# Segment sums moved from TensorE to VectorE in a two-branch transformer kernel, with a new order of tiled products and tail

## The chip, the cores and the metric

The kernel runs on one core of a Trainium2 chip. The metric is the device time of one execution, in microseconds (us). A core has five engines with queues of their own, each executed in order: TensorE (PE, matrix products), VectorE (DVE), ScalarE (ACT), GpSimd (POOL) and SyncE (SP), which here only issues transfers (DMA). POOL issues transfers too. Engines wait for one another through semaphores.

## The reference

The output is the sum of three terms on one input `x` of 2048 tokens by 1024 channels, bf16:

```python
xn = _layernorm(x)
return x + A(xn, mem0, Wq, Wk, Wv, Wo, 32) + B(xn, w1, w2, w3, w4)

# A: recurrent memory attention, 32 heads of 128, segments of 32 tokens
for s in range(64):
    h = concat([mem, xn[segment s]])            # 8 memory tokens + 32
    q, k, v = h @ Wq, h @ Wk, h @ Wv
    p = softmax(where(mask, q @ k.T * scale, -1e9))
    o = (p @ v) @ Wo
    mem = o[:8]; outs.append(o[8:])

# B: token-shift mixer and MLP (width 3584)
h  = gelu(layernorm(xn) @ w1); hs = shift(h) @ w2
x1 = xn + hs
out_B = x1 + gelu(layernorm(x1) @ w3) @ w4
```

## The kernel before

The token axis is cut into 16 tiles of 128 tokens (`NT`), the channels into 8 slabs of 128 (`KT`). The schedule is manual: each engine executes its instructions in the order in which the Python code records them, and a tile pool's buffers add waits where a buffer is used again. Matrix products go to PSUM; most take one of four buffers of the tag `mm`, some one of two larger ones ("A", "B").

*Stage 1* (about 10 to 71 us). Groups of two tiles. DVE computes the layer norm statistics and a normalised tile (`ln_stats`, `ln_apply`), and SP transposes it by a DMA (`dma_trans`, L235; the first tiles go through PE). PE multiplies by w1, eight chains per group (`stage1`, L266), and ACT applies GELU into `hT_all`. ACT also normalises `x` in place (`normalise_x`, L245). From it PE makes segment sums: `seg_sums(n)` multiplies each of the eight slabs of a tile by a 128x4 matrix of ones (L261, `psX`), and ACT copies the result to `xs` (L262). The sums of two tiles stand after the first four chains of the group that follows them.

*Stage 2* (71 to 126 us). Products with w2 (L367), addition of `xn`, second layer norm, a DMA transpose of each tile (L381), and a write of `x1` to memory (`R1`).

*Stage 3* (126 to 528 us). Four blocks `tb` of 512 tokens. Half 0 of a block is 28 GELU chains (L556, ACT at L557), half 1 is 8 chains of 28 products with w4 (L574), which DVE adds to `R1` (L575). `load_R1(n)` loads `R1` and x again, lets POOL add them (L480), lets DVE normalise x (L481) and POOL write it to memory (`xn_scratch`, L482), from where the attention later loads it transposed (L503). Between the chains the function `filler(tb, half, i)` puts products of the memory path: `plan` says which chunk of Wv or Wo is used after which chain (chunks 0 to 3 in half 1 of block 0, then on to half 0 of block 2). Chunk products (L425 `psvb`, L446 `psG`) start from `xb`, which is computed from `xs` at the start of stage 3. They yield the approximate memory states `MZ`.

*Attention* (528 us to the end). Four batches `b` of 512 tokens by eight groups of four heads: 32 steps of 12 chains each, four for Q (L617), four for K (L635), four for V (L644). After given chains (`at(c, f)`) a step does the tiled products of earlier steps: `scores(p)` (L668, `psS`) and `soft(p)` of the step before, and `values(pp)` (L708 `psO`, L709 `psE`) of the one before that. `soft` is a row of DVE operations with POOL copies at the end (`PT` L695, `BD` L697). `values` is evicted by DVE (L713, L720) and ACT (L715, `mem_values` L731). Weights come in 1 MB transfers (`need_w`, L489). In batch 0, `wo_sb` is loaded as well, 1 MB per step, right after the K weights of the next step (L908). The output products `psP` (L827) of a batch run in the second step of the next; those of the last batch form the tail, in which `out_part(b, c, h0, h1)` does the heads h0 to h1 of one of eight output parts, and a part that is not finished keeps its `mm` buffer.

Of the kernel before, what the change touches and what calls it, by code (L numbers as in the profile page):

```python
# [21 lines left out]
P = 128  # L22
S = 2048
D = 1024
# [39 lines left out]
def kernel(  # L64
# [79 lines left out]
    xs = spec.tile([P, KT, NSEG], F32)  # L144
    xb = spec.tile([P, KT, NG], BF16)
    m0 = spec.tile([M, D], BF16)
    lnst = spec.tile([P, NT, 4], F32)

    rightx = main.enter_context(ExitStack())
# [14 lines left out]
    with ExitStack() as keepx:  # L164
# [6 lines left out]
        with ExitStack() as p0:  # L171
# [83 lines left out]
                        w = 2 if n == 0 else 4  # L255
                        nc.scalar.copy(xn2Ts[n // 2][:, n % 2, 4 * h + q:4 * h + q + w, :], p3_[:, q:q + w, :])

            def seg_sums(n):
                ps = aux_tile([P, KT, 4], "AB"[n % 2], "psX")
                for k in range(KT):  # L260
                    nc.tensor.matmul(ps[:, k, :], xts[n][:, k * P:(k + 1) * P], segone[:], start=True, stop=True)  # L261
                nc.scalar.copy(xs[:, :, 4 * n:4 * n + 4], ps[:])  # L262

            def w1_part(g, co, ps, ks):
                for k in ks:
                    nc.tensor.matmul(ps, w1_sb[:, k, co * P:(co + 1) * P], xn2Ts[g][:, :, k, :], start=(k == 0), stop=(k == KT - 1))  # L266
# [60 lines left out]
            ln_half(5, 1)  # L327
            dma_trans(4)
            single(3, 0)
            seg_sums(0)  # L330
            seg_sums(1)
            normalise_x(2)
            ln_stats(6)
            ln_apply(5)
# [3 lines left out]
            for g in range(2, NT // 2):  # L338
                nxt = [n for n in (2 * g + 2, 2 * g + 3) if n < NT]
                for n in nxt:  # L340
                    if 6 < n + 1 < NT:
                        ln_stats(n + 1)
                    ln_apply(n)
                    dma_trans(n)
                stage1(g, range(4))
                for n in (2 * g, 2 * g + 1):
                    seg_sums(n - 2)
                    normalise_x(n)
                stage1(g, range(4, KT))
            seg_sums(NT - 2)  # L350
            seg_sums(NT - 1)

        x3_pool = rightx.enter_context(tc.tile_pool(name="x3", bufs=1, side="right"))
        w3b_pool = rightx.enter_context(tc.tile_pool(name="w3b", bufs=1, side="right"))
# [34 lines left out]
    with ExitStack() as p3:  # L389
# [9 lines left out]
        for k in range(KT):  # L399
            nc.tensor.matmul(ps9[:, k, :], m0[:, k * P:(k + 1) * P], eye9[:], start=True, stop=True)  # L400
        nc.vector.tensor_copy(MZ[:, :, 0:M], ps9[:, :, 0:M])
        nc.vector.tensor_tensor(xb[:, :, 0:1], ps9[:, :, M:M + 1], xs[:, :, 0:1], op=ALU.add)
        nc.vector.tensor_copy(xb[:, :, 1:NG], xs[:, :, 1:NG])

        chunks = {}

# [11 lines left out]
        def use_chunk(c):  # L418
            t = chunks.pop(c)
            if c < 8:  # L420
                w = t[:].rearrange("p (k e) -> p k e", k=KT)
                ps = aux_tile([P, 4, NG], "A", "psvb")
                for k in range(KT):
                    for hh in range(4):
                        nc.tensor.matmul(ps[:, hh, :], w[:, k, hh * P:(hh + 1) * P], xb[:, k, :], start=(k == 0 and hh == 0),  # L425
                                         stop=(k == KT - 1), skip_group_check=True)
                vb = vbT[:, c * 4:(c + 1) * 4, :]
                nc.vector.tensor_scalar(vb, ps[:], 1.0 / L, None, op0=ALU.mult)
                sq = ring.tile([P, 4, NG], F32, tag="sq", bufs=1, name="sq")
                nc.gpsimd.tensor_tensor(sq[:], vb, vb, op=ALU.mult)  # L430
                for hh in range(4):
                    if c == 0 and hh == 0:
                        nc.gpsimd.tensor_copy(thr[:], sq[:, 0, :])
                    else:
                        nc.gpsimd.tensor_tensor(thr[:], thr[:], sq[:, hh, :], op=ALU.add)
                if c == 7:
                    nc.gpsimd.tensor_scalar(chk[:, NV + 7:2 * NV], thr[:], TOL2, None, op0=ALU.mult)
                    nc.gpsimd.tensor_copy(chk[:, NV:NV + 7], chk[:, NV + 7:NV + 8].to_broadcast((P, 7)))
                return
            c -= 8  # L440
            w = t[:].rearrange("p (h d) -> p h d", h=4)
            if c == 0:
                psG[0] = aux_tile([P, KT, NG], "B", "psG")
            for hh in range(4):
                for k in range(KT):
                    nc.tensor.matmul(psG[0][:, k, :], w[:, hh, k * P:(k + 1) * P], vbT[:, c * 4 + hh, :],  # L446
                                     start=(c == 0 and hh == 0 and k == 0), stop=(c == 7 and hh == 3), skip_group_check=True)
            if c == 7:
                nc.vector.tensor_copy(MZ[:, :, M:NZ], psG[0][:])
# [1 line left out]
        plan = {}  # L451
        slots = {}
        for i in range(4):
            plan[(0, 1, 2 * i + 1)] = i
            plan[(1, 0, 7 * i + 6)] = 4 + i
            plan[(1, 1, 2 * i + 1)] = 8 + i
            plan[(2, 0, 7 * i + 6)] = 12 + i
        for c in range(16):
            slots[c] = 0 if c < 8 else c % 2

        def filler(tb, ph, i):
            c = plan.get((tb, ph, i))
            if c is None:
                return
            use_chunk(c)
            nx = c + 2 if c >= 8 else c + 1
            if c == 7:
                load_chunk(8, slots[8])
                load_chunk(9, slots[9])
            elif c < 7 or nx < 16:  # L470
                load_chunk(nx, slots[nx])
# [3 lines left out]
        def load_R1(n):  # L475
            R1 = ring.tile([P, D], F32, tag="R1", name="R1")
            nc.sync.dma_start(R1[:], R1_v[:, n, :])
            xt = ring.tile([P, D], BF16, tag="xt", name="xt", bufs=2)
            nc.sync.dma_start(xt[:], x_v[:, n, :])
            nc.gpsimd.tensor_tensor(R1[:], R1[:], xt[:], op=ALU.add)  # L480
            nc.vector.tensor_scalar(xt[:], xt[:], lnst[:, n, 0:1], lnst[:, n, 2:3], op0=ALU.subtract, op1=ALU.mult)  # L481
            nc.gpsimd.dma_start(xn_v[:, n, :], xt[:])  # L482
            R1s[n] = R1

        A = {}
# [65 lines left out]
        for tb in range(4):  # L551
            for f in range(FT):
                ps = mm_tile("ps3")
                w3 = w3a if f < FH else w3b
                for k in range(KT):
                    nc.tensor.matmul(ps[:], w3[:, k, (f % FH) * P:(f % FH + 1) * P], xn3Ts[tb][:, :, k, :], start=(k == 0), stop=(k == KT - 1))  # L556
                nc.scalar.activation(h3T[:, f, :], ps[:], ACTF.Gelu_apprx_tanh)  # L557
                filler(tb, 0, f)
                if f == 20:
                    load_R1(tb * 4)  # L560
            if tb == 0:
                load_chunk(0, 0)
            if tb == 3:
                rightx.close()
                att_open()
            for j in range(4):
                n = tb * 4 + j
                if j < 3:
                    load_R1(n + 1)
                R1 = R1s.pop(n)  # L570
                for ch in range(2):
                    ps = mm_tile("ps4")
                    for f in range(FT):
                        nc.tensor.matmul(ps[:], h3T[:, f, j * P:(j + 1) * P], w4t[f // 4][:, f % 4, ch * 512:(ch + 1) * 512], start=(f == 0), stop=(f == FT - 1))  # L574
                    nc.vector.tensor_tensor(R1[:, ch * 512:(ch + 1) * 512], ps[:], R1[:, ch * 512:(ch + 1) * 512], op=ALU.add)  # L575
                    filler(tb, 1, 2 * j + ch)
                nc.gpsimd.dma_start(R_v[:, n, :], R1[:])
                if tb == 3 and j == 0:
                    att_prep()
# [278 lines left out]
    for i in range(NS):  # L858
# [8 lines left out]
            hooks.setdefault(c, []).append((f, a))  # L867

        if p is not None:
            at(7, scores, p)  # L870
        if pp is not None:
            at(7, values, pp)
            at(10, mem_values, pp)
        if 4 < s.hg and s.b + 1 < NB:
            for k in range(3 * s.hg - 15, min(3 * s.hg - 12, KT)):
# [3 lines left out]
            at(8, first_soft, p)  # L879
            at(11, first_trans, p)  # L880
        if p is not None:
            at(11 if fz else 7, soft, p)
        if pp is not None and pp.b == 0:
            at(1, first_values, pp)
        if s.hg == 1 and s.b > 0:
# [11 lines left out]
        for c in range(12):  # L897
            if c < 4:
# [5 lines left out]
                if c == 3:  # L904
                    if i + 1 < NS:
                        need_w("k", i + 1)
                    if s.b == 0:
                        nc.sync.dma_start(wo_sb[:, hsl(s.hg), :], Wo_v[:, hsl(s.hg), :])  # L908
                    if s.hg == 4 and s.b + 1 < NB:
                        load_xT(s.b + 1)  # L910
            elif c < 8:
                k_chain(s, c - 4)
                if c == 7 and i + 1 < NS:
                    need_w("v", i + 1)
            else:
                v_chain(s, c - 8)
                if c == 11:
                    if s.b == 0:
                        mem_proj(s, "v", VM)
                    if i + 2 < NS:  # L920
                        need_w("q", i + 2)
            for f, a in hooks.get(c, ()):
                f(*a)
        if last:
            b = s.b
            load_Rt(b, 0)
            load_Rt(b, 1)
            hp = H - 4
            scores(s)
            values(p)  # L930
            soft(s)
            out_part(b, 0, 0, hp)
            mem_values(p)
            out_part(b, 1, 0, hp)
            values(s)
            out_part(b, 2, 0, hp)
            mem_values(s)
            out_part(b, 0, hp, H)
            out_part(b, 1, hp, H)
            out_part(b, 2, hp, H)  # L940
            out_chain(b, 3)
            mem_add(b)
            compare(b)
            finite()
# [134 lines left out]
```

## Time and profile before

| | us |
|---|---|
| median of 4 runs (lowest to highest) | 1485.36 (1483.96 to 1486.18) |
| the profiled execution | 1485.04 |
| its span, first to last instruction | 1483.3 |
| PE busy | 1473.0 (99%) |
| DVE busy | 513.9 (35%) |
| ACT busy | 347.0 (23%) |
| POOL busy | 205.4 (14%) |

The profile is of one execution. "L266" is line 266 of the kernel before. The slices of the profile are fortieths of the span, 37 us each, and a digit is the busy share in tenths. "PEld" is the loading of weights into PE, which overlaps its products. A wait is put down to the instruction that ended it, the "releaser"; "issue" stands for time in which the engine waited for nothing that the profile shows. The chain is followed back from the last instruction, at each step to what released it or to the instruction before it on the same engine. "To landing" is the time from the issue of a transfer to its completion.

### The profile page before, as it was taken

To read this page: it belongs to the slowest core of one execution; us is meant where nothing else is said; L and a number is where in the kernel's file an instruction comes from. 1 tells how busy PE (TensorE), PEld (TensorE's weight loads), DVE (VectorE), ACT (ScalarE), POOL (GpSimd) and SP (SyncE) were. 2 spreads that over 40 slices of the span, in tenths; PEclk is the share of its full clock that TensorE was granted. 3 is DMA by queue.
4 is the path that set the end of the run, shared out by engine and by line. 5 is a ranking of instruction groups with operands and counts; after the bars stand their busy time and mean duration, and the time that the engine had idled before them with its cause. 6 is when DMAs were issued, how large, how long until landed. Compare 5 with 4: busy or idle time off the path is not lost.

```text
span 1483.3 us, 28434 instructions
## 1 busy us (share of the span) xinstructions
PE 1473.0 (99%) x12384; PEld 755.7 (51%) x12384; DVE 513.9 (35%) x1194; ACT 347.0 (23%) x887; POOL 205.4 (14%) x479
## 2 busy tenths in 40 slices
PE   8999999999999999999999999999999999999998
PEld 7844444444444456666544444444444444444444
DVE  8183010010110213546441354541255542154452
ACT  5633202103113023333320232220122220032210
POOL 6042131211120201111100000000000000000000
PEclk9999999999999999999999999999999999999999
DMA  8599753454120745565531354541345452245301
GB/s 222 137 272 240 257 192 100 161 169 160 57 106 3 230 138 180 164 205 166 170 112 54 121 171 143 157 143 53 103 148 167 143 157 72 71 141 154 105 17 58
DMA packets 189395, 208.40 MB, mean 141 GB/s; under 512 B 50426, under 2 KB 158074, under 8 KB 189266
## 3 DMA queue, kind: packets, MB, share of 16 engines
q1 hardware_dynamic: 181122, 178.97, 40.2%
q0 software_dynamic: 8144, 27.56, 5.2%
q8 instruction: 99, 1.62, 0.5%
q14 instruction: 30, 0.25, 0.1%
HBM read 170.07 MB, written 25.17 MB: 132 GB/s over the span
## 4 chain that ended last, share of the span: by engine, by line
PE 98%; DVE 1%; DMA 0%; issue 0%; SPq 0%; ACT 0%; POOL 0%; POOLq 0%; DVEq 0%
PE psK L635 15%; PE psP L827 15%; PE psQ L617 15%; PE psV L644 14%; PE ps L556 13%; PE ps L574 13%; PE ps L367 4%; PE ps L266 3%; PE psS L668 1%; PE psO L708 1%; PE psM L653 1%; PE psvb L425 1%; PE psG L446 1%; PE ps L295 0%; DMA x<-in_A_x_dram 0%; PE ps L281 0%
## 5 line engine op out<-in xcount | busy, mean ns | idle before, releaser
L827 PE MATMUL psP<-wo_sb,oX 128*128 128x512 bf16 (+2 forms) x1056 | 222.1, 373 | 0.0
L574 PE MATMUL ps<-w,hT_all 128*128 128x512 bf16 x896 | 195.0, 379 | 0.0
L635 PEld LDWEIGHTS <-w 128*128 128x128 bf16 x1280 | 125.1, 98 | 99.1
L644 PE MATMUL psV<-w,xT 128*128 128x512 bf16 x768 | 170.3, 379 | 0.0
L617 PE MATMUL psQ<-xT,w 128*128 128x512 bf16 x768 | 169.9, 379 | 0.0
L635 PE MATMUL psK<-xT,w 128*128 128x512 bf16 x768 | 169.7, 379 | 0.0
L827 PEld LDWEIGHTS <-oX 128*128 128x128 bf16 x1056 | 101.9, 98 | 118.8
L617 PEld LDWEIGHTS <-w 128*128 128x128 bf16 x1024 | 98.9, 98 | 116.6
L636 ACT CAST K<-psK 128x512 bf16<-128x512 f32 (+1 forms) x160 | 80.4, 502 | 303.0 <-PE psK L635 303.0
L645 ACT CAST V<-psV 128x512 bf16<-128x512 f32 x128 | 74.9, 585 | 289.9 <-PE psV L644 289.8
L574 PEld LDWEIGHTS <-hT_all 128*128 128x128 bf16 x896 | 87.1, 98 | 103.8
L624 DVE TENSOR_TENSOR Q<-psQ,QM 128x512 bf16<-128x512 f32 (+1 forms) x128 | 87.5, 685 | 144.1 <-PE psQ L617 92.3
L557 ACT ACTIVATE hT_all<-ps 128x512 bf16<-128x512 f32 x112 | 66.8, 597 | 283.4 <-PE ps L556 283.4
L644 PEld LDWEIGHTS <-xT 128*128 128x128 bf16 x768 | 74.1, 98 | 84.7
L556 PE MATMUL ps<-xn3T,w3a 128*128 128x512 bf16 x448 | 97.7, 379 | 0.0
L556 PE MATMUL ps<-xn3T,w3b 128*128 128x512 bf16 x448 | 97.7, 379 | 0.0
L713 DVE TENSOR_TENSOR oX<-psE,VM 128x128 bf16<-128x128 f32 x32 | 9.3, 292 | 217.7 <-PE psE L709 217.7
L720 DVE TENSOR_TENSOR oX<-psO,VM 128x96 bf16<-128x96 f32 (+2 forms) x256 | 82.1, 394 | 0.0
L833 DVE TENSOR_TENSOR ot<-psP,Rt 128x512 bf16<-128x512 f32 (+2 forms) x33 | 22.3, 676 | 168.9 <-PE psP L827 166.0
L481 DVE TENSOR_SCALAR xt<-xt,lnst 128x1024 bf16<-128x1024 bf16 x16 | 8.7, 546 | 179.8 <-POOL R L480 179.8
L556 PEld LDWEIGHTS <-w3b 128*128 128x128 bf16 x448 | 43.5, 98 | 52.0
L556 PEld LDWEIGHTS <-w3a 128*128 128x128 bf16 x448 | 43.5, 98 | 51.7
(159 smaller groups left out, 1267.3 us busy)
## 6 DMA issues: line engine op xcount, KB each, us to landing
w<-in_A_Wq_dram SPq DMA_DIRECT2D x32, 1024.0 KB, 5.3
w<-in_A_Wk_dram SPq DMA_DIRECT2D x32, 1024.0 KB, 5.3
w<-in_A_Wv_dram SPq DMA_DIRECT2D x32, 1024.0 KB, 6.5
R_scratch<-x POOLq DMA_DIRECT2D x16, 512.0 KB, 7.9
R<-R_scratch SPq DMA_DIRECT2D x16, 512.0 KB, 7.0
chunk<-in_A_Wv_dram SPq DMA_DIRECT2D x8, 1024.0 KB, 5.5
R_scratch<-R POOLq DMA_DIRECT2D x16, 512.0 KB, 3.9
chunk<-in_A_Wo_dram SPq DMA_DIRECT2D x8, 1024.0 KB, 6.7
```

Source lines behind the costliest of these rows:

```text
L367: nc.tensor.matmul(ps[:], hTB[:, k, o:o + P], w2_sb[:, k, ch * 512:(ch + 1) * 512], start=(k == 0), stop=(k == KT - 1))
L556: nc.tensor.matmul(ps[:], w3[:, k, (f % FH) * P:(f % FH + 1) * P], xn3Ts[tb][:, :, k, :], start=(k == 0), stop=(k == KT - 1))
L557: nc.scalar.activation(h3T[:, f, :], ps[:], ACTF.Gelu_apprx_tanh)
L574: nc.tensor.matmul(ps[:], h3T[:, f, j * P:(j + 1) * P], w4t[f // 4][:, f % 4, ch * 512:(ch + 1) * 512], start=(f == 0), stop=(f == FT - 1))
L617: nc.tensor.matmul(ps[:], w[:, k, hh * P:(hh + 1) * P], s.xm[:, k, 0:512], start=(k == 0), stop=(k == KT - 1))
L624: nc.vector.tensor_tensor(q3[:, j0:16, 0:SEG], p3_[:, j0:16, :], QM[:, 4 * s.hg + hh, z + j0:z + 16].unsqueeze(2).to_broadcast((P, 16 - j0 ...
L635: nc.tensor.matmul(ps[:, 0:c], w[:, k, hh * P:(hh + 1) * P], s.xm[:, k, h2 * c:(h2 + 1) * c], start=(k == 0), stop=(k == KT - 1))
L636: nc.scalar.copy(s.K[:, hh, h2 * c:(h2 + 1) * c], ps[:, 0:c])
L644: nc.tensor.matmul(ps[:], s.xm[:, k, m * P:(m + 1) * P], w[:, k, :], start=(k == 0), stop=(k == KT - 1))
L645: nc.scalar.copy(s.V[:, m, :], ps[:])
L720: nc.vector.tensor_tensor(oX[:, h0:h0 + hn, :].rearrange("p h (m c) -> p m h c", c=P)[:, m0:m1, :, SEG * j:SEG * (j + 1)], o4[:, 4 * m0:4 ...
L827: nc.tensor.matmul(ps[:, 0:w], oX[:, h, m * P:(m + 1) * P], wo_sb[:, h, cc], start=(h == 0), stop=(h == H - 1))
```

## The change

- `seg_sums` no longer runs on PE in stage 1. In stage 3 x is loaded and normalised by itself (`load_xn`, `make_xn`), tiles 0 to 9 in half 0 of block 0, tiles 10 to 15 in half 0 of block 1, each loaded two hooks ahead of its use. The transposed block of 512 tokens is loaded into the buffer `x0` (`load_sum`), and DVE reduces over the 32 tokens of each segment, two slabs at a time (`seg_sums`, four per block).
- `xb` is computed after the last sums (`last_sum`), and chunk 0 is loaded then. All chunks move on by one half of a block.
- `load_R1` no longer normalises or writes x. The `xt` tag has three buffers.
- In the attention `scores`, `values` and, where it stood there too, `soft` move from after chain 7 to after chain 6; the load of `wo_sb` moves from after chain 3 to after chain 7.
- In the tail the first 24 heads of part 0 stand ahead of `scores(s)`, and parts 0 to 3 are cut differently.
- The squares for `thr` on POOL are made head by head.

```diff
-            def seg_sums(n):
-                ps = aux_tile([P, KT, 4], "AB"[n % 2], "psX")
-                for k in range(KT):
-                    nc.tensor.matmul(ps[:, k, :], xts[n][:, k * P:(k + 1) * P], segone[:], start=True, stop=True)
-                nc.scalar.copy(xs[:, :, 4 * n:4 * n + 4], ps[:])
...
                 for n in (2 * g, 2 * g + 1):
-                    seg_sums(n - 2)
                     normalise_x(n)
...
-        nc.vector.tensor_tensor(xb[:, :, 0:1], ps9[:, :, M:M + 1], xs[:, :, 0:1], op=ALU.add)
-        nc.vector.tensor_copy(xb[:, :, 1:NG], xs[:, :, 1:NG])
+        nc.vector.tensor_copy(m0s[:], ps9[:, :, M:M + 1])
...
-                sq = ring.tile([P, 4, NG], F32, tag="sq", bufs=1, name="sq")
-                nc.gpsimd.tensor_tensor(sq[:], vb, vb, op=ALU.mult)
+                sq = ring.tile([P, NG], F32, tag="sq", bufs=1, name="sq")
...
-                        nc.gpsimd.tensor_tensor(thr[:], thr[:], sq[:, hh, :], op=ALU.add)
+                        nc.gpsimd.tensor_tensor(sq[:], vb[:, hh, :], vb[:, hh, :], op=ALU.mult)
+                        nc.gpsimd.tensor_tensor(thr[:], thr[:], sq[:], op=ALU.add)
...
-            plan[(0, 1, 2 * i + 1)] = i
-            plan[(1, 0, 7 * i + 6)] = 4 + i
-            plan[(1, 1, 2 * i + 1)] = 8 + i
-            plan[(2, 0, 7 * i + 6)] = 12 + i
+            plan[(1, 1, 2 * i + 1)] = i
+            plan[(2, 0, 7 * i + 6)] = 4 + i
+            plan[(2, 1, 2 * i + 1)] = 8 + i
+            plan[(3, 0, 7 * i + 6)] = 12 + i
...
+        def load_xn(n):
+            xns[n] = ring.tile([P, D], BF16, tag="xt", name="xn", bufs=3)
+            nc.sync.dma_start(xns[n][:], x_v[:, n, :])
+
+        def make_xn(n):
+            xt = xns.pop(n)
+            nc.vector.tensor_scalar(xt[:], xt[:], lnst[:, n, 0:1], lnst[:, n, 2:3], op0=ALU.subtract, op1=ALU.mult)
+            nc.gpsimd.dma_start(xn_v[:, n, :], xt[:])
+
+        def load_sum(b):
+            sums[b] = x3_pool.tile([P, KT * 512], BF16, tag="x0", name=f"xTs{b}")
+            nc.sync.dma_start_transpose(sums[b][:].rearrange("p (k t) -> p k t", k=KT), xn_d[b * 512:(b + 1) * 512, :])
+
+        def seg_sums(b, k0):
+            nc.vector.tensor_reduce(xs[:, k0:k0 + 2, 16 * b:16 * b + 16], sums[b][:].rearrange("p (k s i) -> p k s i", k=KT, i=SEG)[:, k0:k0 + 2, :, :], axis=AX.X, op=ALU.add)
+
+        def last_sum():
+            nc.vector.tensor_tensor(xb[:, :, 0:1], m0s[:], xs[:, :, 0:1], op=ALU.add)
+            nc.vector.tensor_copy(xb[:, :, 1:NG], xs[:, :, 1:NG])
+            load_chunk(0, 0)
...
+        for n in range(10):
+            do(0, 0, 7 + 2 * n, load_xn, n)
+            do(0, 0, 9 + 2 * n, make_xn, n)
+        do(0, 1, 6, load_xn, 10)
+        do(0, 1, 7, load_xn, 11)
+        for n in range(10, NT):
+            do(1, 0, 2 * n - 20, make_xn, n)
+            if n + 2 < NT:
+                do(1, 0, 2 * n - 20, load_xn, n + 2)
+        for b, pos in enumerate(((0, 1, 1), (1, 0, 4), (1, 0, 12), (1, 0, 20))):
+            do(*pos, load_sum, b)
+            for t in range(4):
+                do(1, 0, 8 * b + t, seg_sums, b, 2 * t)
+        do(1, 0, 27, last_sum)
...
             nc.gpsimd.tensor_tensor(R1[:], R1[:], xt[:], op=ALU.add)
-            nc.vector.tensor_scalar(xt[:], xt[:], lnst[:, n, 0:1], lnst[:, n, 2:3], op0=ALU.subtract, op1=ALU.mult)
-            nc.gpsimd.dma_start(xn_v[:, n, :], xt[:])
...
-            at(7, scores, p)
+            at(6, scores, p)
...
-            at(7, values, pp)
+            at(6, values, pp)
...
-            at(11 if fz else 7, soft, p)
+            at(11 if fz else 6, soft, p)
...
-                    if s.b == 0:
-                        nc.sync.dma_start(wo_sb[:, hsl(s.hg), :], Wo_v[:, hsl(s.hg), :])
...
                 if c == 7 and i + 1 < NS:
                     need_w("v", i + 1)
+                if c == 7 and s.b == 0:
+                    nc.sync.dma_start(wo_sb[:, hsl(s.hg), :], Wo_v[:, hsl(s.hg), :])
...
+            out_part(b, 0, 0, hp - 4)
             scores(s)
             values(p)
             soft(s)
-            out_part(b, 0, 0, hp)
+            out_part(b, 1, 0, hp - 4)
             mem_values(p)
-            out_part(b, 1, 0, hp)
+            out_part(b, 0, hp - 4, hp)
+            out_part(b, 1, hp - 4, hp)
+            out_part(b, 2, 0, hp)
             values(s)
-            out_part(b, 2, 0, hp)
+            out_part(b, 3, 0, hp)
             mem_values(s)
...
-            out_chain(b, 3)
+            out_part(b, 3, hp, H)
```

`hp` is 28; p is the step before the last, s the last; `fz` is true where the step before is in batch 0.

## The prediction

> **What bounds the kernel now.** I read the page first: the busy shares by slice, the granted clock, and the chain that ended last.
>
> ```profile
> PE   8999999999999999999999999999999999999998
> DVE  8183010010110213546441354541255542154452
> ...
> PEclk9999999999999999999999999999999999999999
> ...
> PE 98%; DVE 1%; DMA 0%; issue 0%; SPq 0%; ACT 0%; POOL 0%; POOLq 0%; DVEq 0%
> ```
>
> TensorE (PE) is the bound in every slice, at full clock. So a change gains what it takes out of PE's queue and the idle times that it removes, and loses the waits it puts in front of PE. The second view is the list of PE's waits:
>
> ```profile
> PE psO L708 <- POOL PT L695: 0.9, 1, 0.9
> PE psO L708 <- issue: 0.6, 1, 0.6
> PE ps L266 <- ACT hT_all L268: 0.5, 1, 0.5
> PE psV L644 <- issue: 0.3, 1, 0.3
> ```
>
> After the start-up these four, 2.3 us, are all of PE's idle time. Third, the chain in order of time, in the first stage (30 to 45 us) and, second fence, in the tail:
>
> ```profile
> 29.99 2.85 PE ps L266 x26
> 32.84 0.02 issue
> 32.87 0.39 ACT hT_all L268
> 33.26 0.06 issue
> 33.32 3.65 PE ps L266 x32
> 36.98 0.38 PE psX L261 x16
> 37.36 7.01 PE ps L266 x64
> 44.37 0.38 PE psX L261 x16
> ```
>
> ```profile
> 1420.92 0.22 DVE MT L694
> ...
> 1421.29 0.26 POOL PT L695
> ...
> 1421.59 0.62 PE psO L708 x60
> ```
>
> A pair of segment sums (`psX`, 16 products) takes 0.38 us of PE. In the tail the second `values` stands 0.93 us because the softmax before it ends in PT on GpSimd (POOL). Last, the stall at 32.84 us: which transfer came then? The transposes issued at 25 to 26 us are one, tile 7's:
>
> ```profile
> L235 SPq DMA_TRANSPOSE xn2T<-xn x1: 1232/1232/1232, 25.5 to 25.5; - x1
> ...
> DMA to landing us min/median/max: 7.7/7.7/7.7
> ```
>
> It landed at 25.5 + 7.7 = 33.2 us, and PE went on at 33.32. The products of group 3 read that tile, so this wait has a floor that is not ACT's.
>
> **The change, part by part.** Sums are made against the profiled execution, 1485.04 us (span 1483.3 and 1.7 around it). The median of the runs, 1485.36, is 0.3 higher, which I add at the end. 0.2% is 3.0 us: about what a measurement of this kernel can tell from no change.
>
> *Segment sums off PE.* Eight pairs of 0.38 us leave, 3.0 us. Two of them stand before the stall at 32.84. Tile 7's transpose hangs on VectorE's (DVE) normalising and on the SP queue, which the change leaves alone there, so it still lands at 33.2: PE comes 0.76 us earlier and waits 0.76 us longer. The later groups have room: group 4 will want tile 9 at 33.3 + 7.0 = 40.3 us, and tile 10, behind it in the queue, landed at 39.9; tile 11 was there at 44.2, for group 5 at 47.3. So six pairs count: 6 x 0.38 = **-2.3 us** (bounds -3.0, if the transpose lands sooner, and -2.0). The 16 PSUM copies of 0.18 us that leave ACT cost nothing and free nothing that ends last.
>
> *The tail.* `scores`, `values` and `soft` come one chain (1.73 us) sooner, and 24 products of `psP` (5.2 us) now stand in front of `scores(s)`. The softmax needs 9.7 us from the start of psS (1411.82) to PT (1421.55). Between the same points PE now has 1.34 (psS, psO, psE), 1.73 (a K chain), 6.91 (V), 5.2 and 0.6: 15.8 us. The wait goes, -0.93. What is late next: part 3 of the output now starts straight after psE. Parts 0, 1 and 2 hold three of the four `mm` buffers, so it needs psE's own, which is free only after DVE has read it (0.29, L713) and ACT too (0.16, L715). The first psE ended at 1422.38 on the chain and L715 at 1422.90. With 0.05 for the semaphore that is 0.58 us, on the path. In the kernel before, part 2 found a free buffer there. Last, `soft(s)` gave BD 9.1 us after psE (1422.2 to 1431.3), and 13.0 us of products will cover it. Together **-0.35** (bounds -0.93, and +0.3 if the new wait takes 1.2).
>
> *Products in all other steps one chain sooner.* Same instructions, 1.34 us per step. They need soft of the step before: in batch 0 BD was ready 13.7 us before psO, and one chain of that is given up. The psK that follows needs the buffer of two chains ago, evicted within 0.6 us under 1.34 us of products: nothing.
>
> *`wo_sb` load moved.* The two "issue" waits (0.60 at 666.1 us, 0.32 at 617.9) lie just behind psS and psO, which take 250 PE instructions in 1.3 us. Both fall in batch 0, in steps where 1 MB of `w` and 1 MB of `wo_sb` were issued together 7 us earlier:
>
> ```profile
> 658.02 0.37 SPq L489 DMA_DIRECT2D w<-in_A_Wk_dram  x1
> 658.44 0.58 SPq L908 DMA_DIRECT2D wo_sb<-in_A_Wo_dram  x1
> ```
>
> I read them as PE's instruction fetch (1.62 MB in 99 packets on q8, for 24,768 products and weight loads: some 250 in a packet) held up by those 2 MB. In the 24 steps after batch 0 only 1 MB of weights is under way there, and none of them has such a wait. With `wo_sb` behind the products it is 1 MB in batch 0 as well, though the products now stand only 5.3 us behind its issue (three chains of 1.77), just its landing time. I take **-0.8** of the 0.92 (bounds -0.92 and +0.3: three stalls of 0.4).
>
> The Trainium skill ("Runtime: NRT & Kernel Launch", Instruction fetch mechanics) also has blocks of 256 instructions, but calls the fetch mostly hidden. By that rule this term would be 0 and the sum -2.6; the two "issue" rows speak against it.
>
> *Normalised x made sooner, in GELU chains.* The 16 steps on DVE (0.546 us, L481) and the POOL-issued writes (0.58) move from the second half of each block to the first two; x is read twice. None is PE's. New waits, in time of the kernel before, since transfers and PE both shift: SP has three `xt` buffers, and behind its waits stands the load of R1 for tile 0. The first three x loads queue behind w4 and land by 169.5, when the same 768 KB of R1 and xt had landed (L480 began at 169.57). Their writes land 2.3 us after issue: 172.6. The second round, at the median landing of xt, 4.3 (2.3 to 9.6 over the 16), ends 4.3 + 0.65 + 2.4 later, at 180.0. Then R1 lands 6.2 later (the least from 100 to 300 us), POOL adds for 2.1 (188.3), tile 6's write behind it is down at 191.2, and tile 9 loads and is normalised by 196.1. Only then does DVE evict the first `ps` of L574, 0.7 us. PE needs that buffer for its fifth chain, at 174.8 + 4 x 6.04 = 199.0. I take cost 0: the cover is 2.2 us, and 6.3 at the least landing, to which a queue without other loads is nearer.
>
> *Sums on DVE.* 16 reductions of 128x1024 bf16. The nearest row:
>
> ```profile
> L677 DVE TENSOR_REDUCE ss<-EQ 128x16 f32<-128x528 f32 x32 | 22.5, 703 | 2.7
> ```
>
> 528 elements in 703 ns and 32 in 186 (L689) give 1.04 ns an element, so 1.22 us each, 20 us in all, inside 48 us of GELU chains in which DVE has nothing that PE waits for. The upper bound is the strided row L790, 1015 ns for 512: 2.0 us. They run in series with the transposes, since all four blocks share one buffer: 6 us for block 0 from 223.9, then three times 8.6 (median landing of L503, 6.1 to 12.2) + 5.0, last sum 0.6, chunk 0 landed 5.6 later: 277. psvb first reads it at 223.2 + 48.35 + 12.1 = 283.7. Cost 0, cover 6.7 us. Chunks then come every 12 us as before. The longer chain of small POOL operations per chunk (2.4 us for 1.8) lies in those 12 us.
>
> Sum: -2.3 - 0.35 - 0.8 = -3.4 us: 1481.6 profiled, **1481.9 us** median.
>
> **Rivals.**
>
> *The x loads hold DVE, and PE waits for PSUM (slower).* Place: the fifth chain of L574 in block 0. Each microsecond of landing time beyond the above counts twice. At the 6.9 us that xt took beside R1 and chunk loads (median from 100 to 300 us), with R1 at its 8.0, tile 9 is ready at 203.1 and PE stands 4.8 us: +1.4, 1486.8. It decides for slower (over +3.0) from 7.7 us per load; at the longest, 9.3, PE stands 9.6: 1491.6. For it: SP, DVE and POOL are all in order here. Against: after 170 us no other load shares the queue.
>
> *The sums come late.* Place: psvb of chunk 0. If transposes take 12.2 us (one of four did, behind two weight loads): 4.1 us late, 1486.1. With 2.0 us reductions as well: 16.6 late, 1498.6.
>
> *Less gain.* The fetch waits stay or move, or the new wait behind psE is longer: -1 to -2.8 us, 1482.6 to 1484.4.
>
> *All eight pairs count*: the transpose of tile 7 is not the floor, 1481.2.
>
> **How the numbers follow.** The forecast's case has 0.52 (1480.4 to 1482.9; 0.46 of it under 1482.4, 0.06 above). Less gain 0.18 (same). All pairs 0.08 (faster). Late x loads 0.14 (0.11 slower, 0.03 same). Late sums 0.08 (0.07 slower, 0.01 same). So faster 0.54, same 0.28, slower 0.18. The range goes from all terms at their better bounds (-4.9, 1480.5) to the mild case of the late x loads, 1486.8; what lies beyond is the 0.18.
>
> **What would show it.** Right: no psX on PE; PE's stall near 33 us grown to about 1.2 us and ended by the same transpose; PE reaching L367's stage 2.3 us sooner; no wait for PT at the tail, a new one of about 0.6 us at psP on ACT's read of psE; no "issue" wait in batch 0. Wrong: a wait of PE at the `ps` of block 0's second half (released by DVE), or at psvb; "issue" waits in batch 0; a stall near 33 us that did not grow.

## The result, and the profile after

The changed kernel takes **1483.51 us** (median of 37 runs, 1481.17 to 1485.61) against 1485.39 us (57 runs, 1483.90 to 1494.18) for the kernel before. The ratio is 0.9986, 95% interval 0.9981 to 0.9990. So it is 1.9 us faster by the medians (1.5 to 2.8 by the interval): real, under the 0.2% that I had named as the bound, and 1.6 us short of the forecast of 1481.9. A second set of times (experiment 9) gave 0.998, interval 0.9967 to 0.9993.

The profiled execution of the changed kernel took 1485.81 us with a span of 1483.8: it is longer than each of the 37 runs, and 0.8 us longer than that of the kernel before. It must be read with that in mind; what made it long is the first finding. The page, with the rows that were shown of before:

```profile
PE   8999999999999999999999999999999999999998
...
DVE  7184114210000213546441364540245532154442
...
PEclk9999999999999999999999999999999999999999
...
PE 64%; DMA 0%; issue 0%; DVE 0%; ACT 0%; ACTq 0%
```

PE is still the bound in every slice. The chain covers only 64% because it is followed back no further than 530.93 us: the first `psQ` chain stood 0.10 us (535.88 to 535.99) for a write of R. The page's tenths hide the rest. The list of PE's waits shows it (total us, times, longest):

```profile
PE ps L261 <- DMA xn2T<-xn: 2.6, 1, 2.6
...
PE psP L859 <- ACT oT L747: 0.6, 1, 0.6
...
PE psK L667 <- issue: 0.2, 1, 0.2
```

Of the four waits after the start-up that the kernel before had, the one for PT (0.93) is gone, the two "issue" waits (0.92 together) have become one of 0.16, and a wait of 0.57 behind psE is there as forecast. But the stall near 33 us is 2.56 us, not 1.2. The transpose of tile 7 was issued at 25.67 us and took 9.4 us to land, where it had taken 7.7 before:

```profile
L236 SPq DMA_TRANSPOSE xn2T<-xn x1: 1233/1233/1233, 25.7 to 25.7; - x1
...
DMA to landing us min/median/max: 9.4/9.4/9.4
```

And the stall cost more than itself. Busy time by stretch, the same kernel; the number behind the five engines' times is the granted clock:

```profile
32.00:33.00 1.00, 0.67 (x7) 0.35 (x4) 0.96 (x5) 0.96 (x4) 0.54 (x1) 1.00 2.52 131
33.00:34.00 1.00, 0.00 (x0) 0.00 (x0) 1.00 (x2) 0.09 (x1) 0.66 (x2) 1.00 0.84 28
...
36.00:37.00 1.00, 1.00 (x9) 0.72 (x6) 0.97 (x3) 0.38 (x1) 0.00 (x0) 0.63 1.11 365
37.00:38.00 1.00, 1.00 (x6) 0.73 (x5) 0.96 (x5) 0.12 (x1) 0.48 (x1) 0.50 1.00 373
...
40.00:41.00 1.00, 1.00 (x11) 0.90 (x10) 1.00 (x3) 0.42 (x2) 0.61 (x2) 1.00 1.15 320
```

From 36.26 us on PE ran at half clock for 3.41 us: its 128x256 products stood 213 ns apart instead of 109. That is about 1.7 us more: 16 products at 0.104, and from the end of the stall to the start of stage 2 it took 36.60 us here and 34.93 in experiment 7, which has the same stage 1 at full clock. The products' count in the row (6 and 7 for 11) says it too, while the row of busy tenths shows nothing. In this execution stage 2 began at 71.82 us, 1.2 us *later* than before (70.66), although 3 us of products had left.

### The profile page after: what moved, and what is told of

The parts are those of the page before. It is cut to its first block, busy times and chain, and to the rows that moved or that the text cites. A ratio compares the mean times of both kernels' runs of the same rounds, so it can differ in the third digit from the quotient of the medians.

```text
span 1483.8 us, 28244 instructions
## 1 busy us (share of the span) xinstructions
PE 1472.5 (99%) x12256; PEld 753.4 (51%) x12256; DVE 534.8 (36%) x1211; ACT 345.6 (23%) x871; POOL 207.0 (14%) x502
## 4 chain that ended last, share of the span: by engine, by line
PE 64%; DMA 0%; issue 0%; DVE 0%; ACT 0%; ACTq 0%
PE psK L667 15%; PE psP L859 15%; PE psV L676 15%; PE psQ L649 15%; PE psS L700 1%; PE psO L740 1%; PE psM L685 1%; PE psE L741 0%; DMA R_scratch<-R 0%; PE psZO L805 0%; PE psZ L784 0%; PE psZT L798 0%; ACT QM L687 0%; ACTq L687 0%; DVE oX L745 0%
## 5 line engine op out<-in xcount | busy, mean ns | idle before, releaser
L667 PE MATMUL psK<-xT,w 128*128 128x512 bf16 x768 | 173.6, 379 | 0.0
L607 DVE TENSOR_TENSOR R<-ps,R 128x512 f32<-128x512 f32 x32 | 22.1, 691 | 164.0 <-PE ps L606 153.7
```

The source lines that it names most:

```text
L667: nc.tensor.matmul(ps[:, 0:c], w[:, k, hh * P:(hh + 1) * P], s.xm[:, k, h2 * c:(h2 + 1) * c], start=(k == 0), stop=(k == KT - 1))
```

## The experiments

All edits are to the changed kernel unless said otherwise. A ratio is that to the kernel before on the same chip, and the two numbers behind it are its 95% interval. Three questions were open: is the stall near 33 us a rule or a chance; do the other two terms hold; where is the rest of the forecast's gain?

**1. Two of the eight pairs put back.** After `single(3, 0)` and beside `normalise_x` of group 2 stand again

```diff
+            seg_products(0)
+            seg_products(1)
...
+                    if g == 2:
+                        seg_products(n - 2)
```

> The changed kernel with two pairs of the old segment products (32 products of 25 ns, 0.76 us of PE, their sums used by nobody) put back where they stood before the stall near 33 us. Forecast's theory (the stall ends when tile 7's transpose lands, whatever PE did before): PE stops 0.76 us later, starts again at the same time, stage 2 begins at the same time, 1483.5 us. Clock theory (a stall of 2.5 us makes the granted clock fall to 0.5 for 3.4 us, as in the changed kernel's profile from 36.2 to 39.6 us, at a price of 1.7 us): the stall is 0.76 us shorter, the fall comes in fewer executions, 1482.3 to 1483.3 us. Rival (the stall is no floor): the products cost what they take, 1484.3 us.

Measured 1483.35 us, ratio 0.9982 (0.9967 to 0.9998): no dearer than the changed kernel. Stall 1.79 us at full clock, transpose 8.95 us, stage 2 at 69.04. This fits both the floor and the clock and excludes neither; only the rival (1484.3) is further off, though the interval holds it too. It showed an "issue" wait of 0.87 us with the *late* `wo_sb` load, so that wait isn't gone, only rarer.

**2. Tile 7 transposed by PE.**

```diff
-                    dma_trans(n)
+                    if n != 7:
+                        dma_trans(n)
                 stage1(g, range(4))
+                if g == 2:
+                    pe_trans(7)
```

> The changed kernel with tile 7 transposed by eight PE products of 76 ns (0.61 us) in the middle of group 2's chains instead of by a DMA transpose. Forecast's theory: the stall (forecast at 1.2 us) goes for 0.6 us of products, 1482.9 us. Clock theory: the stall of 2 to 2.6 us goes, and the half clock behind it (1.7 us where it comes), less 0.6 us: 1480.8 to 1482.0 us, no granted clock below 1 after the start, stage 2 beginning near 68.7 us (70.66 before, less 3.0 for the segment products, less 0.5 for the stall, plus 0.6, plus 0.9 as the changed kernel's PE stood at 25.47 when the one before stood at 25.24 with a pair more behind it). Rival: another transpose (tile 9's) takes tile 7's place as the wait, stage 2 no earlier than 70 us, 1483.0 us or more.

The median was 1488.97 us (1482.14 to 1497.4, ratio 1.0013, 0.9987 to 1.0039), and no theory had its reason. The stall near 33 us was gone and stage 2 began at 68.29, but at its end PE stood for a small constant:

```profile
PE ps L393 <- DMA c_eye_sb<-c_eye: 10.2, 1, 10.2
```

This load stands at stage 2's ninth tile in SP's queue, behind weights and transposes; it was issued at 124.8 us here, 1.1 us after PE came for it, and at 107 to 112 us in most profiles. The clock was at half from 126.20 to 139.85 us, 6 us beyond the wait's end, which cost some 3 us more. Seven of the twelve times lay at 1486.7 to 1497.4, the profiled one (1495.9) among them, and five at 1482.1 to 1483.1.

**3 and 4. The change in halves.** Experiment 3 puts the old attention part (the `wo_sb` load, the hooks at 7, the old tail) into the changed kernel; experiment 4 puts the new one into the kernel before.

> The changed kernel with the attention part of the kernel before (wo_sb load behind the third q chain, scores, values and soft at the seventh chain, the old tail); segment sums stay on DVE. Forecast's theory: the PT wait of 0.9 us and the issue waits of 0.9 us in batch 0 come back, the wait for ACT's read of psE goes: +1.15, 1484.7 us. Rival (these waits were chance or moved): 1483.5 us.

> The kernel before with the attention part of the changed one only; segment sums stay on PE, stage 1 as before. Forecast's theory: -1.15 from 1485.4, 1484.2 us, stall near 33 us still about 0.5 us at full clock. If the attention part gives more and stage 1 nothing: 1483.5 us; if less: 1485.4 us.

Measured 1484.04 us (ratio 0.9988, 0.9972 to 1.0003) and 1484.01 us (0.9988, 0.9973 to 1.0004), against 1485.05 for the kernel before on that chip: each half gave 1.0 us by the medians, and the intervals are too wide for more. The traces say more. Experiment 3's list of PE's waits has the three old ones back and no stall at all at 33 us, with the same stage 1 that had 2.56 in the changed kernel:

```profile
PE psO L740 <- POOL PT L727: 0.9, 1, 0.9
PE psV L676 <- issue: 0.9, 1, 0.9
...
PE psO L740 <- issue: 0.6, 1, 0.6
```

Its transpose of tile 7 took 6.33 us, that of experiment 4 5.91, and neither stalled. So the changed stage 1 doesn't bring the long stall by rule: it comes with a late landing.

**5 and 6. Versions with the new tail wait mended.** Part 3 waited because psE's buffer was the only one left. Both versions put four heads' products behind the second `values`:

```diff
-            out_part(b, 2, 0, hp)
+            out_part(b, 2, 0, hp - 4)
             values(s)
+            out_part(b, 2, hp - 4, hp)
             out_part(b, 3, 0, hp)
```

Experiment 5 adds experiment 2's edit, with the c_eye load moved to stage 2's first tile; experiment 6 is this edit alone.

> The changed kernel with three edits: tile 7 transposed by PE; the load of c_eye moved from stage 2's ninth tile to its first (in the kernel with tile 7 on PE alone, PE stood 10.2 us for it at 123.7 us); and in the tail the last four heads' products of part 2 (4 x 0.216 = 0.86 us) put behind the second values, where they cover the 0.57 us that part 3 waits for psE's buffer. Clock theory (stall near 33 us plus half clock cost the changed kernel some 1.7 us on the median, PE's transpose 0.6): the undisturbed executions with tile 7 on PE had 1482.4, less 0.57: 1481.8 us, no stall near 33 us, no wait for c_eye, no wait behind psE. Forecast's theory (a stall of 1.2 and nothing else): 1483.5 - 0.6 - 0.57 = 1482.3 us. Rival: the late transfers of stage 2 stop PE at another place (the first chains of stage 3, by xn3T or w3a): 1488 us or more.

> The changed kernel with only the tail's edit: the last four heads of part 2 behind the second values. Forecast's reading (psE's buffer is what part 3 waits for): the 0.57 us wait at psP goes, 1482.9 us. Rival: it moves to psE, which would now wait for BD (12.1 us of products before it for the 9.1 us that BD takes): 1483.5 us or more.

Measured 1482.53 us (0.9981, 0.9972 to 0.9991) and 1482.68 us (0.9985, 0.9975 to 0.9995), with 1485.67 for the kernel before. Neither profile has a wait at psP or psE any more: the reading of the buffer was right. Experiment 5 had no stall and no wait for c_eye, but its PE began the second set of transposes late (11.56 us; 10.71 in the changed kernel), so stage 2 began at 69.07. Its median lies above both theories' figures (1481.8 and 1482.3), its interval (1481.5 to 1484.3) holds both, and so it doesn't tell them apart. Experiment 6's profiled execution is the undisturbed one: transpose 6.6 us, no stall, no "issue" wait, stage 2 at 67.02, 1479.9 us.

```profile
L236 SPq DMA_TRANSPOSE xn2T<-xn x1: 1232/1232/1232, 25.4 to 25.4; - x1
...
DMA to landing us min/median/max: 6.6/6.6/6.6
```

**7 and 11. The `wo_sb` load back behind the third q chain**, nothing else; 11 is a second profile of the same kernel.

> The changed kernel with only the wo_sb load back behind the third q chain. Forecast's theory: the issue waits of batch 0 return, 0.9 us in place of 0.1, 1484.3 us. Rival (the waits scatter from run to run and have nothing to do with this load; a run with the late load showed one of 0.87 us): 1483.5 us.

> The changed kernel with the early wo_sb load once more, for a second profile: its 11 times had a median 2.2 us above the changed kernel's, more than the 1.5 us of issue wait in its profile. Forecast's theory: issue waits in batch 0 of 0.9 to 2.5 us in all, the late load's are 0 to 0.9. Rival: they are under 0.5 us and the time lies elsewhere.

Measured 1486.01 us (0.9997, 0.9980 to 1.0013) and, in a single run, 1486.13: by the medians the whole gain of the change is lost again, more than forecast (1484.3). The interval is wide enough to hold the changed kernel's 0.9986 too, but on the same chip experiment 6, which has the late load and the tail's edit (0.57 us), took 1482.68. The "issue" waits were 1.62 us in the first profile. In the second:

```profile
PE psK L667 <- issue: 1.9, 1, 1.9
...
PE psV L676 <- issue: 0.9, 1, 0.9
```

The longer one was followed by a half clock of 3.41 us. These waits are longer than in the kernel before, where the products stood one chain further behind the load.

**8. Holes made on purpose.** Between GELU chains of blocks 2 and 3 PE waits for 6 to 33 small VectorE operations in series, 14 times:

```diff
+            nc.vector.tensor_copy(t[:], h3T[:, f, 0:64])
+            for _ in range(k):
+                nc.vector.tensor_scalar(t[:], t[:], 1.0, None, op0=ALU.mult)
+            nc.tensor.matmul(ps[:, 0:64], ident[:], t[:], start=True, stop=True)
```

> The changed kernel with 14 holes made on purpose between GELU chains of blocks 2 and 3: behind a chain's GELU, VectorE makes a copy and 6 to 33 small operations on it in series, and PE waits for the last. Clock theory: behind holes of about 2.5 us and more the granted clock is 0.5 for 3.41 us and the next products take twice as long, 1.7 us; behind holes under 1.8 us never; between them it depends on where the hole lies in windows of 3.41 us. Rival (the half clock in the changed kernel's profile had another cause than the idle time, such as the work just behind it): no hole is followed by a half clock, or all are alike. The time is the sum of the holes and says nothing else.

The holes were 2.26 to 8.05 us long (1577.43 us in all). Not their length alone decided. Two of them, and the stretch behind each (the clock is again the number behind the engines):

```profile
348.30:352.00 3.70, 0.13 (x3) 0.08 (x3) 2.37 (x13) 0.60 (x1) 0.00 (x0) 1.00 0.00 0
352.00:355.30 3.30, 3.30 (x17) 1.53 (x18) 0.00 (x0) 0.60 (x1) 0.00 (x0) 1.00 0.02 5
523.50:526.70 3.20, 0.13 (x2) 0.04 (x2) 2.00 (x11) 0.60 (x1) 0.00 (x0) 1.00 1.01 393
527.80:531.10 3.30, 3.30 (x9) 1.21 (x8) 0.00 (x0) 0.60 (x1) 3.30 (x2) 0.50 0.27 103
```

A hole of 3.57 us (348.36 to 351.93) left the clock alone; one of 3.07 us (523.59 to 526.66) halved it. All changes of the clock in a trace lie on one grid of 3.413 us, and the idle time *within one grid window* sorts them: in dense chains at full clock, windows with up to 1.93 us idle were followed by full clock and windows with 2.31 us or more by half clock, over the 14 profiles, with none between. The changed kernel's window had 2.38. The rival falls; the theory's figure of 2.5 us a hole was too simple.

**9 and 10. Both kernels once more**, for second profiles.

> The changed kernel once more, for a second profile of it and a second set of times. Scatter theory (tile 7's transpose lands 5.9 to 9.4 us after its issue, by chance; PE reaches it 6.6 to 7.2 us after): the stall near 33 us differs from the 2.56 us of the first profile, most often under 1 us and with no half clock behind it; ratio to the kernel before 0.9975 to 0.999. Rival (the removal of the products makes the long stall and the half clock the rule): a stall of 2 us or more and a half clock again.

> The kernel before once more, for a second profile of it. Scatter theory: the stall near 33 us is 0 to 2 us (0.49 in the first), the issue waits in batch 0 add up to 0.9 to 1.6 us, the wait for PT is 0.93 again; the last PE product is followed by 4.4 to 4.8 us of span and no instruction load after its end; time less span 1.7 to 1.8 us.

Measured 1482.96 us (0.998, 0.9967 to 0.9993) and 1485.67 (1.0001, 0.9988 to 1.0013). The kernel before showed a stall of 1.08 us (transpose 8.3), issue waits of 0.91 and the PT wait of 0.92. The changed kernel showed a stall of 1.30 at full clock: under the rival's 2 us and without its half clock, though not under the 1 us that the scatter theory held for the most frequent. That execution took 1490.91 us all the same, for experiment 2's wait, now in the changed kernel itself, and for a half clock from 127.80 to 134.62 us, 4.4 us of it behind that wait:

```profile
PE ps L390 <- DMA c_eye_sb<-c_eye: 6.5, 1, 6.5
...
PE ps L261 <- DMA xn2T<-xn: 1.3, 1, 1.3
```

**12. The tail's edit, and x's third tile ahead of w1's second pair.**

```diff
             load_w1(0)
-            load_w1(2)
             load_x(2)
+            load_w1(2)
```

> The changed kernel with the tail's edit and with the third tile of x loaded ahead of the second pair of w1 rows. In the profiles x's third tile landed at 8.4 to 10.3 us, VectorE's second tile of normalised x and PE's second set of transposes followed it one to one (9.6 to 11.6 us), and all of stage 1 moved with them. Theory: it lands by 7.7 us, the transposes begin near 9.5, stage 2 near 67 us when tile 7 lands in time: 0.9 us less than with the tail alone, 1481.8 us. Rival: w1's second pair, now later, stops the first products as long: 1482.7 us, PE waits for w_sb near 9 us.

Measured **1481.64 us** (ratio 0.9979, 0.9968 to 0.9990), the lowest median of all; the changed kernel had 1482.96 on the same chip, so it beats the kernel before, and the changed one by 1.3 us on the medians without an interval between the two. VectorE had the second tile at 9.35 us (10.35 in experiment 6), but PE's transposes began only at 10.15: part of the gain went into a new wait for w1, as the rival said, and stage 2 began at 68.12, since the transpose of tile 7 was late this time:

```profile
PE ps L261 <- DMA xn2T<-xn: 1.3, 1, 1.3
PE ps L276 <- DMA w_sb<-in_B_w_dram: 0.4, 1, 0.4
```

The profiles side by side (us; experiments 1, 2, 5 and 12 have another stage 1, and 8 is left out of the last column):

| kernel | tile 7, issue to landing | stall near 33 | stage 2 begins | issue waits, batch 0 | last landing to end of span | time less span |
|---|---|---|---|---|---|---|
| before | 7.70 | 0.49 | 70.66 | 0.92 | 1.79 | 1.77 |
| before again (10) | 8.27 | 1.08 | 71.34 | 0.91 | 1.79 | 1.76 |
| new attention (4) | 5.91 | 0 | 69.07 | 0.27 | 1.79 | 1.76 |
| changed | 9.42 | 2.56, half clock | 71.82 | 0.16 | 2.08 | 2.02 |
| changed again (9) | 7.92 | 1.30 | 68.37 | 0.12 | 2.08 | 1.90 |
| old attention (3) | 6.33 | 0 | 68.00 | 1.47 | 2.08 | 2.03 |
| tail (6) | 6.59 | 0 | 67.02 | 0 | 2.08 | 1.91 |
| early wo_sb (7) | 7.62 | 1.00 | 67.98 | 1.62 | 2.08 | 2.09 |
| early wo_sb (11) | 8.24 | 1.84 | 68.03 | 2.74, half clock | 2.08 | 1.96 |
| holes (8) | 7.42 | 0.80 | 67.94 | 0.45 | 2.08 | – |

## Why the prediction was right, and where it was wrong

The measured 1483.51 us lies in the stated range and is faster, but outside the forecast's own case (1480.4 to 1482.9, chance 0.52). By the number it is in that of the rival "less gain" (1482.6 to 1484.4, 0.18), and "same", which is a change under the 3.0 us of the bound, had 0.28 in all against 0.54 for "faster". The grounds given for that rival weren't what was found: the wait behind psE was 0.57 as forecast, and in the changed kernel's two profiles the "issue" waits of batch 0 were 0.16 and 0.12.

**The bound, and what hides under it: right.** PE stayed the bound. The 16 sums on VectorE took 1.21 us each (1.22 forecast):

```profile
L468 DVE TENSOR_REDUCE xs<-xTs x16: 1208/1211/1221, 225.4 to 267.1; 128x32 f32<-128x1024 bf16 x16
```

They were done at 268.3 us, and `psvb` began at 284.59 without a wait. VectorE was through with the tenth tile of normalised x at 187.4 and evicted the first `ps` of block 0's second half then, 5.4 us after its chain's end; PE needed the buffer at 200.0. So neither rival on the slower side showed in any profile, and the cover of the x loads was 12 us, not 2.2 (in the second round the loads whose landing the trace tells took 3.0 to 3.2 us, for the 4.3 assumed).

**The segment sums, -2.3: right as a mean, wrong as a constant.** The step said that tile 7 lands at 33.2 whatever PE does. It lands 5.9 to 8.3 us after its issue with the old stage 1 and 6.3 to 9.4 with the new one, and PE comes to it 7.3 us after the issue with the old stage 1 and 6.5 to 7.0 with the new one. With the kernel before's stage 1 the stalls were 0.49, 1.08 and 0 (mean 0.52), with the changed one 2.56, 1.30, 0, 0, 1.00, 1.84 and 0.80 (mean 1.07), and one half clock of 1.7 in seven (0.24). The growth, 0.55 + 0.24 = 0.79 us, is all that the first two pairs free, and leaves the forecast's six: 8 x 0.38 - 0.79 = 2.25. Stalls that scatter so leave the growth uncertain by about half a microsecond, so an agreement to 0.1 is luck; nor is it shown whether the change itself makes tile 7 land later. Stage 2 begins at 70.36 on the mean of three and 68.45 of seven, -1.9; another part of the scatter comes with x's third tile, which moves the start of stage 1 by up to 1.4 us. What the prediction missed here is the price of a long stall: it had taken a wait at its own length.

**The tail, -0.35: right.** 0.93 went and 0.57 came, by the buffer that was named.

**The wo_sb load, -0.8: right.** With the early load and the old hooks the waits were 0.92, 0.91 and 1.47 (mean 1.10); with the late load, in nine profiles, 0.16, 0.12, 0.27, 0, 0.45, 0.87, 0.49, 0.45 and 0 (mean 0.31): -0.8. They did not go altogether, and seven of the nine profiles have one in batch 0, which the prediction had named as a sign of being wrong: the size was right, the clean end was not. The zero cost of the hooks one chain sooner is the part that was wrong if taken alone: with the early load they made the waits 1.6 to 2.7 us. The Trainium skill ("Runtime: NRT & Kernel Launch", Instruction fetch mechanics) has the fetch mostly hidden. Mostly holds here, since at most two of a run's 98 or 99 instruction packets on q8 were followed by such a wait in batch 0; but a load moved by four chains moves these waits by 0.8 to 2.4 us.

That the wait is the fetch, the traces support more strongly than the prediction did. All 16 "issue" waits of PE over 0.1 us in batch 0, over all profiles, end 1.24 to 1.57 us after a 16 KB instruction packet on q8 has landed, though these packets come some 4 to 18 us apart there (experiment 6). In the kernel before such packets landed at 616.70 and 665.40 us, and the waits ended at 618.23 and 666.74. These packets took no longer than the others in batch 0 (0.97 to 1.15 us; medians 0.99 to 1.13), so what made them late lies before their start. That it is the 2 MB under way rests on the place of the load alone.

**The end: left out, and this is a step that failed.** The sum held 1.7 us around the span and everything behind the last product as fixed. In all profiles with the new sums, the span ends 2.08 us after the last output has landed, 2.17 in experiments 2 and 5 (1.79 in the three without): SP has four more semaphores to pass after that landing, 20 for 16. And the time exceeds the span by 2.01 us (median of the changed kernel's runs) for 1.77, with one more 8 KB instruction load 1.8 us behind the span; that this load is the reason isn't shown. Together +0.5 us on the medians; in single runs of the changed kernel the second part lay between 1.71 and 2.13.

With it the profiles' sum is -1.9 (or -2.25 by the terms) - 0.35 - 0.8 + 0.5, that is -2.55 to -2.9, inside the measured -1.5 to -2.8 or just below it. The medians' -1.9 is 0.7 to 1.0 less. This rest is not settled: seven profiles whose stage 2 begins anywhere from 67.0 to 71.8 us can't show it. The late c_eye, in one of the changed kernel's two profiles, is a candidate: PE comes there some 2 us sooner. That the change makes it more frequent wasn't tried, and the 37 runs hold no wait of that size: the longest took 1485.61 us, 2.1 over the median.

## What to carry to other kernels

Work taken off the bound engine ahead of a transfer gives back what the transfer makes it wait, and the transfer's landing is a spread, not a number: take several profiles before a stall of a microsecond is called a floor. Products that run while a DMA is awaited need not be only waste, since a hole past some two thirds of a clock window (2.31 of 3.41 us here) was followed by half clock, 1.7 us more in the changed kernel; experiment 1, which put such products back, couldn't tell. And an edit of "nothing" may be the one that pays or costs: the place of one 1 MB load in each step of batch 0 moved the median by about as much as the whole change.

## What the runs showed of the hardware

- The clock. Half clock came in whole windows of 3.413 us on a grid that started at another phase in each run, after windows with 2.31 us or more without products (1.93 was harmless). The Trainium skill ("TensorE: Matmul & The Clock Gate", Part 1: The HAM clock gate) has the same free-running window of 3413 ns, but puts the return to half clock behind a whole idle window; here a stall of 2.56 us was enough where 2.38 of it lay in one window, and 3.57 us wasn't where it lay across two (1.91 and 1.66). One exception: in experiment 11 a window with 1.56 us idle was followed by half clock; its other products were the short ones of the scores and values.
- DMA transposes of the same 256 KB tile took 5.9 to 9.4 us to land. In their slow stretches, 26 to 34 us into the run, packets of 256 B took up to some 150 ns on the mean of a microsecond (235 once), for 18 elsewhere. What slows them stayed open.
- A tiny load of a constant came 6.5 and 10.2 us late in two of fourteen profiles: it stood behind transposes that SP took 8.0 and 8.3 us to issue, where most took 1.3 to 4 us (the kernel before had one of 8.5 us too, behind that load).
